# First pair of an attention and gated-MLP kernel rebuilt: keys ahead of values, scores in token halves, q turned by products, x scaled by a diagonal product, one output transfer a tile

## Chip, cores and metric

One core of a Trainium2 chip. The metric is the device time of one execution in microseconds, median of several runs; a run of this kernel can be told from another where they differ by about 0.2%. Engines: PE (TensorE, matrix products; PEld its weight loads), DVE (VectorE), ACT (ScalarE), POOL (GpSimd), SP (SyncE, which issues all DMAs here).

## The reference

```python
def _attn_ref(q, k, v, phi):              # each (8 batches, 8 heads, 576 tokens, 64); phi (.., 32)
    a = np.exp(phi - np.max(phi, axis=2, keepdims=True))
    a = a / (np.sum(a, axis=2, keepdims=True) + 1e-09)
    k_m = np.einsum('bhsm,bhsd->bhmd', a, k)
    v_m = np.einsum('bhsm,bhsd->bhmd', a, v)
    scores = np.matmul(q, k_m.transpose(0, 1, 3, 2)) / np.sqrt(64)
    scores = np.exp(scores - np.max(scores, axis=-1, keepdims=True))
    attn = scores / (np.sum(scores, axis=-1, keepdims=True) + 1e-09)
    return np.matmul(attn, v_m)
...
x = attn_out.transpose(0, 2, 1, 3).reshape(4608, 512)
xn = x / np.sqrt(np.mean(x * x, -1, keepdims=True) + 1e-06) * rms_g
g = xn @ w_gate                            # 512 x 1536, float64 in memory
out = (g / (1 + np.exp(-g)) * (xn @ w_val)) @ w_out
```

Each head has 32 memory slots, so keys and values are first condensed to 32 rows a head; everything after that works on a (tokens x 256 slots of 8 heads).

## The kernel before

**Stages.** Batches go in four pairs. For each batch the kernel makes e = exp(phi - max) (`prep`: maximum mc, two small transposes mt and mr, difference phi, exponential e_bd, partial sums es), then key and value summaries kvp (`kv_steps`: 72 products, the sums, factors si and im, spread tiles kb and vb, turned to kvt and copied as km and vt; vt times rms_g is vm, vt times vt is gram). For each pair it turns q (qtp, copied as qT), makes scores S, subtracts their maximum (mxs, ex), takes exp and divides by the total (sm) to get a. `x_steps` turns a (tp, copied as at), makes sums of squares by way of gram (xp, ssq), inverse norms rinv by Newton steps (`fin`), spreads these over partitions (rp), multiplies at, and splits the product into a high and a low part for exact enough fp32r products (ath, atl).

**Main pass.** 48 columns of 128 hidden units in an order given by ORDER, the first eight for the first pair. A column i has `vw_steps` (vp: weights wc folded with vm, split into xh and xl; the bank of vp is single, so the next vp waits for both xl), `gv_steps` (pg and pv, each three products of high and low parts, for two groups of tokens, 256 and 320 columns; then sg = silu, hf = pv * sg, its high part hh and low part hl), and for each second column `out_steps` (po: six products of 512 columns for each of nine token tiles, added to acc by DVE; when a pair ends, `put` sends acc to memory in two transfers of 64 partitions). "Main pass" below is the time from the first pv or pg on. The weights come as float64 words (raw) and are converted by `convert` on ACT, DVE and POOL (wex, mi, wc, w, oh, ol), then kept in DRAM for later pairs.

**What sets the order.** All steps are small functions in one list, and ISSUE (L31) is a table of their numbers: `perform` calls them in that order, and every engine takes its instructions strictly in that order. Buffers come from pools; a tile whose tag has no free buffer waits for the release of the oldest. Before, L318 loads keys and values of a head pair into one tile (kv, eight buffers), L535 loads all of q of a head pair into the same buffers, and q is copied into another order by ACT (L545) and transposed, nine transposes a head pair. Scores of a head pair take 576 columns in the double bank vw. es is made on POOL (L406), atl too (L778), and hl (L1069).

**Lines used below.** L350 mc, L378 mr, L387 phi, L396 e_bd, L436 kvp products, L448 kvp sums, L472 kb and vb, L487 and L517 kvt, L545 the copy of q, L557 turn of q, L578 S, L591/L595/L606/L612 softmax of the first pair, L665 to L691 that of later pairs, L759 rp, L767 at * rp, L794 xp, L806 squares, L911 to L948 weight conversion, L1002 vp, L1018 xl, L1038 pg and pv, L1054 hf, L1064 hh, L1069 hl, L1095 po, L1104 acc, L1108 output transfers.

## Time and profile before

| | |
|---|---|
| median of 3 runs | 834.62 us (833.40 to 834.71) |
| the profiled execution | 833.51 us, its span 831.7 us, mean granted clock 0.982 |
| busy share | PE 95%, PEld 81%, DVE 55%, ACT 44%, POOL 32% |
| moved by DMA | 120 MB, mean 144 GB/s |
| chain that ended last | PE 84%, DVE 6%, ACT 3%, DMA 3% |

A row of a timeline gives start and duration in us, engine, line, operation, out<-in, shapes, count and in brackets the idle time of the engine before it with what ended it. A row of groups ends with "busy us, mean ns | idle before, and what ended it". PE and PEld overlap, and a row of PE is longer than the spacing of products that follow each other. fp32 products are two records each, transposes and fp32r products one.

### The profile page before, as it was taken

How to read it: one execution, taken by the hardware profiler on the slowest of the kernel's cores; microseconds unless marked ns; L12 is line 12 of the kernel's file. 1: busy time of each engine (PE TensorE's matmuls, PEld its weight loads, DVE VectorE, ACT ScalarE, POOL GpSimd, SP SyncE). 2: the span in 40 equal slices, each digit the busy share in tenths (PEclk: the TensorE clock that was granted, in tenths of full speed). 3: DMA queues.
4: the chain of work that ended last, by engine and by line, in shares of the span. 5: the costliest groups of instructions: out<-in, count | busy, mean ns of one | idle time of the engine just before them, and what ended most of it. 6: DMA issues, size and time to landing. Idle time of an engine off the chain costs nothing.

```text
span 831.7 us, 19077 instructions
## 1 busy us (share of the span) xinstructions
PE 788.9 (95%) x7903; PEld 672.6 (81%) x7903; DVE 459.2 (55%) x1014; ACT 364.0 (44%) x683; POOL 264.7 (32%) x223
## 2 busy tenths in 40 slices
PE   3866999999999999999999999999999999999996
PEld 2654888787988888888888788888888888888884
DVE  4497668899762566555655333556544432444443
ACT  1565688754654646322354247542332244232220
POOL 1255555555542324211153113122241122122220
PEclk9697999999999999999999999999999999999999
DMA  9856677665573450753345454450232433211114
GB/s 322 284 196 223 202 198 220 201 223 197 197 241 102 139 177 21 229 163 110 100 134 171 136 146 109 106 181 32 77 102 73 117 115 127 69 59 52 51 52 114
DMA packets 99327, 120.00 MB, mean 144 GB/s; under 512 B 47908, under 2 KB 64680, under 8 KB 99240
## 3 DMA queue, kind: packets, MB, share of 16 engines
q1 hardware_dynamic: 99240, 118.78, 45.8%
q8 instruction: 62, 1.02, 0.5%
q14 instruction: 25, 0.20, 0.1%
HBM read 93.19 MB, written 25.56 MB: 143 GB/s over the span
## 4 chain that ended last, share of the span: by engine, by line
PE 84%; DVE 6%; ACT 3%; DMA 3%; issue 2%; SPq 1%; POOLq 0%; POOL 0%; DVEq 0%; ACTq 0%
PE po L1095 34%; PE pg L1038 18%; PE pv L1038 17%; PE vp L1002 6%; PE kvp L436 2%; PE xp L794 2%; PE S L665 2%; DMA raw<-in_moe_w_val_dram 1%; PE qtp L647 1%; DMA kv<-in_v_dram 1%; PE tp L739 1%; DVE xl L1018 1%; DVE wex L915 1%; DVE wex L934 1%; DVE mc L350 1%
## 5 line engine op out<-in xcount | busy, mean ns | idle before, releaser
L1069 POOL TENSOR_TENSOR hl<-hf,hh 128x512 fp32r<-128x512 f32 (+1 forms) x96 | 137.9, 1440 | 381.3 <-ACT hh L1064 365.2
L1104 DVE TENSOR_TENSOR acc<-po,acc 128x512 f32<-128x512 f32 x180 | 123.0, 688 | 125.3 <-PE po L1095 124.6
L1095 PE MATMUL po<-oh,hh 128*128 128x512 f32 x432 | 174.9, 405 | 1.8 <-DVE acc L1104 0.9
L1095 PE MATMUL po<-oh,hl 128*128 128x512 f32 x432 | 170.7, 395 | 0.9 <-POOL hl L1069 0.9
L1095 PE MATMUL po<-ol,hh 128*128 128x512 f32 x432 | 170.5, 395 | 0.0
L1049 ACT ACTIVATE sg<-pg 128x256 f32<-128x256 f32 (+1 forms) x192 | 77.3, 412 | 182.4 <-PE pg L1038 148.4
L1054 DVE TENSOR_TENSOR hf<-pv,sg 128x256 f32<-128x256 f32 (+1 forms) x192 | 85.0, 453 | 127.2 <-PE pv L1038 71.7
L1064 ACT CAST hh<-hf 128x512 fp32r<-128x512 f32 (+1 forms) x96 | 64.3, 674 | 80.7 <-DVE hf L1054 79.4
L1095 PEld LDWEIGHTS po<-oh,hh 128*128 128x128 f32 x432 | 81.3, 188 | 22.6 <-issue 3.5
L1095 PEld LDWEIGHTS po<-oh,hl 128*128 128x128 f32 x432 | 81.1, 188 | 21.1 <-POOL hl L1069 1.3
L1095 PEld LDWEIGHTS po<-ol,hh 128*128 128x128 f32 x432 | 81.3, 188 | 14.1
L1038 PE MATMUL pg<-ath,xh 128*128 128x256 f32 (+1 forms) x384 | 87.6, 309 | 0.1
L1038 PE MATMUL pv<-ath,xh 128*128 128x320 f32 (+1 forms) x384 | 86.4, 306 | 0.0
L1038 PE MATMUL pv<-ath,xl 128*128 128x320 f32 (+1 forms) x384 | 82.4, 296 | 0.0
L1038 PE MATMUL pg<-ath,xl 128*128 128x256 f32 (+1 forms) x384 | 82.3, 296 | 0.0
L1038 PE MATMUL pv<-atl,xh 128*128 128x320 f32 (+1 forms) x384 | 82.1, 295 | 0.0
L1020 ACT CAST xh<-vp 128x512 fp32r<-128x512 f32 x96 | 54.5, 587 | 62.5 <-PE vp L1002 30.3
L1038 PE MATMUL pg<-atl,xh 128*128 128x256 f32 (+1 forms) x384 | 81.8, 294 | 0.0
L1018 DVE TENSOR_TENSOR xl<-vp,xh 128x512 fp32r<-128x512 f32 x96 | 64.1, 684 | 30.8 <-ACT xh L1020 30.8
L1038 PEld LDWEIGHTS pg<-ath,xh 128*128 128x128 f32 x384 | 63.1, 189 | 11.7 <-issue 4.2
L1038 PEld LDWEIGHTS pv<-ath,xh 128*128 128x128 f32 x384 | 64.1, 190 | 9.4 <-issue 2.3
L1038 PEld LDWEIGHTS pv<-atl,xh 128*128 128x128 f32 x384 | 61.8, 189 | 0.0
(114 smaller groups left out, 1079.7 us busy)
## 6 DMA issues: line engine op xcount, KB each, us to landing
wc<-wd SPq DMA_DIRECT2D x36, 512.0 KB, 4.4
oh<-od SPq DMA_DIRECT2D x36, 256.0 KB, 3.6
ol<-od SPq DMA_DIRECT2D x36, 256.0 KB, 4.0
out_dram<-acc SPq DMA_DIRECT2D x72, 128.0 KB, 3.0
kv<-in_k_dram SPq DMA_DIRECT2D x26, 288.0 KB, 6.1
kv<-in_v_dram SPq DMA_DIRECT2D x26, 288.0 KB, 6.0
qr<-in_q_dram SPq DMA_DIRECT2D x48, 144.0 KB, 3.4
raw<-in_moe_w_val_dram SPq DMA_DIRECT2D x12, 512.0 KB, 3.9
```

What stands on the lines that cost most here:

```text
L436: nc.tensor.matmul(st["kvp", b][cc][to, 0:128], e_of(b)[rows, hp, c, :], st["kv", b, hp][rows, :, 64 * c:64 * c + 64], start=(c == 0), sto ...
L665: nc.tensor.matmul(sp[64 * j:64 * j + 64, 64 * t:64 * t + 64], d["qT"][:, t0 + t, 64 * j:64 * j + 64], st["km", 2 * pr + j][:, s, :], star ...
L1002: nc.tensor.matmul(vp[32 * g:32 * g + 32, flip(b, cc), cc, :], vm[pr][rows, b, hp, 32 * (g % 2):32 * (g % 2) + 32], w[rows, hp, :], start= ...
L1018: V.tensor_tensor(out=xl[:, k], in0=src, in1=xh[:, k].bitcast(F32), op=ALU.subtract)
L1020: nc.scalar.copy(xs[i][0][:, k], src)
L1038: nc.tensor.matmul(pt[:, :N], l[:, flip(b, cc), cc, half * P:half * P + P], r[:, b, cc, t0:t0 + n, :].rearrange("p t x -> p (t x)"), start ...
L1049: nc.scalar.activation(sg[:, :N], acts[gi, b, 0][:, :N], AF.Silu)
L1054: V.tensor_tensor(out=acts[gi][:, :, b, :], in0=acts[gi, b, 1][:, :N].rearrange("p (t x) -> p t x", x=64), in1=acts[gi, b, 2][:, :N].rearr ...
L1064: nc.scalar.copy(hh, acts[gi].rearrange("p t b x -> p t (b x)"))
L1069: nc.gpsimd.tensor_tensor(out=hl, in0=acts[gi].rearrange("p t b x -> p t (b x)"), in1=hsplit[i, gi][0].bitcast(F32), op=ALU.subtract,)
L1095: nc.tensor.matmul(po, l[:, tt, :], r, start=(m == 0), stop=(m == 5))
L1104: V.tensor_tensor(out=accs[key], in0=pt[0], in1=accs[key], op=ALU.add)
```

## The change

Seven edits and a new table:

1. Keys and values of the first pair are loaded and multiplied apart (`load_one`, `kv_steps(b, i)`): keys of both batches first, values later. Factors si and im are made once with the keys (`scale_all`); hmask is laid out for that.
2. q of the first pair is loaded, turned and scored in two parts of the tokens, tiles 0 to 3 and 4 to 8. A turn is no transpose of a reordered copy any more, but two plain products with the identity for each token tile, one for each head, into halves of the partitions. Scores take one bank of tag g for each part.
3. x of the first pair isn't multiplied by spread norms: `scaled` makes diagonal tiles dg of the norms on ACT, multiplies a by them on PE (ts), and splits the bank directly (ath on ACT, atl on DVE). The other pairs keep the old way.
4. es of the first two batches on DVE instead of POOL.
5. hl of the second token group of the first twelve columns on DVE instead of POOL.
6. The first two raw weight blocks have buffers of their own.
7. One output transfer of 128 partitions a tile instead of two of 64.

The ISSUE table is new throughout.

```diff
-    10, 11, 0, 12, 1, 13, 2, 14, 15, 16, 3, 4, 5, 6, 900, 7, 27, 8, 17, 9, 29, 30, 31, 32, 33, 34, 38, 18, 19,
...
+    def load_one(i, b, hp):
+        t = sa.tile([P, S], F32, tag="kv", name=f"{'kv'[i]}{b}_{hp}", bufs=9)
+        load(t, (k, v)[i][b, 2 * hp:2 * hp + 2].rearrange("h (p c) d -> (h p) (c d)", c=NT))
+        st["kv"[i], b, hp] = t
...
-                nc.gpsimd.tensor_tensor(
+                (V if b < 2 else nc.gpsimd).tensor_tensor(
                     out=t, in0=e[:, :, 0:2, :] if c == 2 else t, in1=e[:, :, c:c + 2, :], op=ALU.add
...
+        products = [chunk(c, c + 3) for c in range(0, NT, 3)]
+        if i == 0:
+            return products + [sums, scale_all(), spread(0), spread(1)], [turn(0), put_k]
+        if i == 1:
+            return products + [spread(0), spread(1)], [turn(1), [put_v, gain], self_products, keep]
...
-                    nc.tensor.transpose(
-                        out=tp[:, (t - t0) * P:(t - t0 + 1) * P],
-                        in_=qr[:, t].rearrange("p h d -> p (h d)"), identity=ident,
-                    )
+                    for h in range(2):
+                        nc.tensor.matmul(
+                            tp[64 * h:64 * h + 64, (t - t0) * P:(t - t0 + 1) * P],
+                            qr[:, h, 64 * t:64 * t + 64], ident, start=True, stop=True,
+                        )
...
-            sp = ps.tile([P, 1024], F32, tag="vw", name=f"S0_{s}", bufs=1)
-            for t in range(NT):
+            sp = bank("g", f"S0_{s}_{t0}")
+            for t in range(n):
...
+        def scaled(t0):
+            n = min(2, NT - t0)
+            def diag(t):
+                def f():
+                    d["dg", t] = dg = sa.tile([P, P], F32, tag="dg", name=f"dg{t}", bufs=4)
+                    nc.scalar.activation(dg, ident, AF.Copy, scale=rinv[pr][:, t:t + 1])
+                return f
+            def mm():
+                tps["s", t0] = tp = bank("v", f"ts{pr}_{t0}")
+                for t in range(t0, t0 + n):
+                    for cc in range(2):
+                        o = 2 * (t - t0) + cc
+                        nc.tensor.matmul(
+                            tp[:, o * P:(o + 1) * P], srcs[t][:, cc * P:(cc + 1) * P], d["dg", t],
+                            start=True, stop=True,
+                        )
...
-                nc.gpsimd.tensor_tensor(
+                (V if gi and i < 12 else nc.gpsimd).tensor_tensor(
                     out=hl, in0=acts[gi].rearrange("p t b x -> p t (b x)"),
...
-                for b in range(2):
-                    load(
-                        out[(2 * pr + b) * S:(2 * pr + b + 1) * S].rearrange("(p c) d -> p c d", c=NT)[:, t, :],
-                        accs[key0, t][64 * b:64 * b + 64, :],
-                    )
+                load(
+                    out[2 * pr * S:(2 * pr + 2) * S].rearrange("(q c) d -> q c d", c=NT)[:, t, :],
+                    accs[key0, t],
+                )
...
+    for t0, n in GROUPS:
+        for s in range(HP):
+            add(lambda s=s, t0=t0, n=n: load_q(s, t0, n), q_steps(s, t0 == 0), score_steps(s, t0, n))
+    for b in range(2):
+        add([lambda b=b, hp=hp: load_one(1, b, hp) for hp in range(HP)], *kv_steps(b, 1))
```

The order at three places. First DVE where the scores of the first pair begin, before; the number after a name's first digits tells the head pair, and the last number is the buffer's.

```order
L934 SCALAR_TENSOR_TENSOR wex0_0_459<-raw_00_314,wex0_0_459 128x512
L350 TENSOR_REDUCE mc2_0_546<-phi2_456 128x128
L591 TENSOR_REDUCE mxs0_0_559<-S0_0_523 128x18
L595 TENSOR_TENSOR ex0_0_561<-S0_0_523,mxs0_0_559 128x576
L365 TENSOR_REDUCE mx2_0_564<-mt2_0_548 128x2
L373 COPY mb2_0_568<-mx2_0_564 128x128
L606 TENSOR_REDUCE sm0_0_574<-ex0_0_561 128x18
L591 TENSOR_REDUCE mxs0_1_610<-S0_1_578 128x18
```

DVE at the same place after; the third number of mxs, S and ex is the first token tile of the part.

```order
L491 TENSOR_TENSOR kb1_473<-kvp1_0_319,im1_444 128x128 x2
L491 TENSOR_TENSOR vb0_601<-kvp0_1_476,im0_402 128x128
L640 TENSOR_REDUCE mxs0_0_0_603<-S0_0_0_569 128x8
L644 TENSOR_TENSOR ex0_0_0_605<-S0_0_0_569,mxs0_0_0_603 128x256
L491 TENSOR_TENSOR vb0_601<-kvp0_1_476,im0_402 128x128
L640 TENSOR_REDUCE mxs0_1_0_633<-S0_1_0_589 128x8
L644 TENSOR_TENSOR ex0_1_0_635<-S0_1_0_589,mxs0_1_0_633 128x256
L653 TENSOR_REDUCE sm0_0_0_661<-ex0_0_0_605 128x8
```

The scores follow the summaries of the keys at once; weight conversions and the maximum of batch 2 (mc2) have moved behind them.

Second PE where the main pass begins, before; kvp3 is the summary of batch 3, mr3 a transpose of its prep.

```order
L517 MATMUL kvt2_1091<-vt2_1113 64x64 x4
L1002 MATMUL vp2_1141<-wc2_1002,vm0_469 32x256 x16
L378 MATMUL mr3_0_1165<-ident_72,mb3_0_1058 128x128
L1038 MATMUL pv0_10_1170<-ath0_1103,xh0_847 128x320 x2
L1038 MATMUL pv0_10_1170<-atl0_1108,xh0_847 128x320 x2
L1038 MATMUL pv0_10_1170<-ath0_1103,xl0_882 128x320 x2
```

PE there after.

```order
L462 MATMUL kvp3_0_1346<-ones_109,e_bd1_131 32x1 x4
L462 MATMUL kvp3_1_1347<-ones_109,e_bd1_131 32x1 x4
L1090 MATMUL vp1_1480<-wc1_1208,vm0_639 32x256 x16
L1126 MATMUL pg0_00_1510<-ath0_1152,xh0_1387 128x256 x2
L1126 MATMUL pg0_00_1510<-atl0_1163,xh0_1387 128x256 x2
L1126 MATMUL pg0_00_1510<-ath0_1152,xl0_1393 128x256 x2
```

All of kvp3 now stands ahead of the main pass, vp2 behind its first products. On DVE the last operations that these wait for are now the following, with mc4, the maximum of batch 4, among them.

```order
L864 TENSOR_TENSOR atl0_1163<-ts0_4_1328,ath0_1152 128x2x128 x2
L359 TENSOR_REDUCE mc4_0_1372<-phi4_1308 128x128
L1106 TENSOR_TENSOR xl0_1393<-vp0_1189,xh0_1387 128x512
L864 TENSOR_TENSOR atl0_1163<-ts0_6_1378,ath0_1152 128x2x128
L1106 TENSOR_TENSOR xl0_1393<-vp0_1189,xh0_1387 128x512
```

Before, neither atl nor mc4 was on this list of DVE at this place.

Third PE near the end, before: the last pv of column 47 stands between two output tiles.

```order
L1095 MATMUL po47_3_10188<-oh47_10143,hl47_0_10154 128x512
L1038 MATMUL pv47_11_10200<-ath3_7814,xh47_9931 128x320 x2
L1038 MATMUL pv47_11_10200<-atl3_7963,xh47_9931 128x320 x2
L1038 MATMUL pv47_11_10200<-ath3_7814,xl47_9933 128x320 x2
L1095 MATMUL po47_5_10214<-oh46_10158,hh46_1_10094 128x512
```

PE near the end after.

```order
L1126 MATMUL pv47_11_10397<-ath3_8037,xl47_10210 128x320 x2
L1126 MATMUL pv47_10_10404<-ath3_8037,xh47_10208 128x320 x2
L1126 MATMUL pv47_10_10404<-atl3_8055,xh47_10208 128x320 x2
L1126 MATMUL pv47_10_10404<-ath3_8037,xl47_10210 128x320 x2
L1183 MATMUL po47_0_10413<-oh46_10357,hh46_0_10273 128x512
```

All pg and pv of the last column now stand ahead of its nine output tiles.

More of the change, by code (lines that the diff above doesn't have):

```diff
@@ L864, in x_steps @@
         steps.append(fin(4, NT))
+        if pr == 0:
+            return steps + [scaled(t0) for t0 in range(0, NT, 2)]
         for t0, n in ((0, 4), (4, 4), (8, 1)):
@@ L891, in load_w @@
         j = column(n)
-        t = wp.tile([P, 512, 2], I32, tag="raw", name=f"raw_{kind}{n}", bufs=2)
+        if n < 1 and kind < 2:
+            t = sa.tile([P, 512, 2], I32, tag="raw0", name=f"raw_{kind}{n}", bufs=2)
+        else:
+            t = wp.tile([P, 512, 2], I32, tag="raw", name=f"raw_{kind}{n}", bufs=2)
         if kind == 2:
@@ L1125 @@
     load(st["rg_rows"], rms_g.rearrange("(hp r) -> hp r", r=P))
-    for hp in range(HP):
-        load_kv(0, hp)
     load_phi(1)
-    for hp in range(HP):
-        load_kv(1, hp)
+    for b in range(2):
+        for hp in range(HP):
+            load_one(0, b, hp)
     add(prep(0, 0, 2), prep(0, 2, 4)[:-1], prep(1))
```

168 lines of the change are left out of this document (105 added, 63 removed), and 320 rows, old and new, of the table ISSUE.

## The prediction

> **What bounds the kernel now.** I read the windows first, then the order of time in the two places where TensorE is not full: the head and the last 20 us. The columns are the stretch, its length, busy time of PE, PEld, DVE, ACT and POOL, the granted clock, the DMA share and GB/s.
>
> ```profile
> 0.00:37.15 37.15, 20.25 (x455) 15.78 (x456) 16.58 (x53) 12.31 (x19) 8.64 (x16) 0.81 0.86 296
> 37.15:79.20 42.05, 28.38 (x544) 20.57 (x545) 38.50 (x112) 24.93 (x49) 20.46 (x19) 0.87 0.68 229
> 79.20:208.00 128.80, 125.78 (x1272) 106.88 (x1273) 102.50 (x220) 87.54 (x162) 72.29 (x60) 0.99 0.67 206
> 208.00:811.00 603.00, 601.31 (x5581) 519.45 (x5580) 294.91 (x620) 238.50 (x455) 161.73 (x128) 1.00 0.38 117
> 811.00:831.70 20.70, 13.22 (x57) 9.91 (x55) 6.72 (x10) 0.72 (x1) 1.55 (x1) 0.92 0.50 114
> ```
>
> Between 79.2 and 811 us PE idles 3.0 + 1.7 us: the main pass is bound by TensorE, and nothing in this change takes products out of it. The head (0 to 79.2) holds 30.6 us of idle PE and the tail 7.5. So the span is the start of the main pass, plus the products left then, plus the tail.
>
> The head has two stretches. Up to 37.15 DMAs bring phi, keys, values and q (296 GB/s), and the first maximum of scores waits for them. From there VectorE is busy 38.5 of 42.05 us. These rows of the timeline are the two borders:
>
> ```profile
> 37.15 0.76 DVE L591 TENSOR_REDUCE mxs<-S 128x18 f32<-128x576 f32 x1 [1.90 <-PE S L578]
> ```
>
> ```profile
> 79.20 0.88 PE L1038 MATMUL pv<-ath,xh 128*128 128x320 f32 x2
> ```
>
> **The change part by part.** *The scores start earlier.* Before, the first scores stand behind sixteen key and value transfers, two weight blocks and all of q 0. The weight block of 512 KB issued behind phi (2 x 576 KB) and the sixteen (288 KB each) ends ScalarE's wait here:
>
> ```profile
> 23.56 0.67 ACT L911 ACTIVATE wex<-raw 128x512 f32<-128x512 f32 x1 [2.46 <-DMA raw<-in_moe_w_val_dram]
> ```
>
> That is 6272 KB by 23.5 us, 267 KB/us from zero. After, the first scores need both batches' keys, the first half of q 0 and, since PE takes them in order, the values of batch 0. Up to the last of these SP issues 1152 of phi, 8 x 288 of keys, 4 x 256 + 320 of q and 4 x 288 of values: 5952 KB, at 22.3 us. Then PE runs the 72 value products of batch 0, one turn of q and the turn of the keys of batch 1:
>
> ```profile
> 20.55 1.12 PE kvt L487 x4
> 21.67 4.29 PE kvp L436 x141
> ```
>
> The 141 records of 128 columns took 4.29 us; 144 of 64 columns cost between half of that and all of it. I take 2.2 (the columns halve), plus 0.6 for two of four kvt, plus 1.2 for eight products of the turn (below), plus 0.3 for scores: 22.3 + 4.3 = 26.6 us, so 26.5, between 25 and 28.5. Before it was 37.15.
>
> *The turn of q.* The copy L545 goes; it runs on ScalarE, busy 24.9 of 42 us, and costs nothing once the scores have begun. A turn is now two plain products into 64-partition halves instead of one transpose. The nearest row is xp, with the same shape (72 records are 36 products):
>
> ```profile
> L557 PE MATMUL qtp<-ident,qr 128*128 128x128 f32 x36 | 8.1, 359 | 1.8 <-ACT qT L563 1.8
> ```
>
> ```profile
> L794 PE MATMUL xp<-gb,at 128*64 128x128 f32 x72 | 5.3, 282 | 3.1 <-DVE ssq L806 1.7 <-ACT at L749 1.4
> ```
>
> A product is 5.3 / 36 = 0.147 us, 72 of them 10.6 against 8.1: 2.5 us more, in PE time that idles; if the idle were gone, 2.5 us later. Eight of them are 1.2 us on the path, counted above.
> The Trainium skill speaks against this edit: TensorE: Matmul & The Clock Gate, section Terms, calls the transpose mode 4 times faster for FP32, and TensorEngine Tiling (Array Packing), section Restrictions, says that column tiling turns it off. By that an eighth of the turns, 0.9 us as transposes, would cost 3.6 instead of 1.2, the scores would start 2.4 us later, and the sum below would be 8.3 instead of 10.7; the xp row puts the ratio for this shape at 10.6 / 8.1, and I use the row.
>
> *VectorE's list from the first maximum to the start of the main pass.* Before, it ends with the product of x and the spread norms (L767), at 76.1. After, PE's last product ahead of the main pass, vp1, needs the bank of vp0, so it waits for the second xl0. Between these borders the two lists differ, at these means of 37.15 to 76.1:
>
> ```profile
> L934 DVE SCALAR_TENSOR_TENSOR wex<-raw,wex 128x512 int32<-128x512 int32 x6 | 4.6, 761 | 0.0
> L806 DVE CUSTOM_DVE_ANT_0 xp<-xp,a 128x256 f32<-128x256 f32 x9 | 3.7, 433 | 0.0
> L915 DVE TENSOR_SCALAR wex<-wex 128x512 f32<-128x512 f32 x7 | 3.5, 513 | 1.0 <-ACT wex L911 0.9
> L591 DVE TENSOR_REDUCE mxs<-S 128x18 f32<-128x576 f32 x4 | 3.0, 756 | 1.9 <-PE S L578 1.9
> L595 DVE TENSOR_TENSOR ex<-S,mxs 128x576 f32<-128x576 f32 x4 | 3.0, 752 | 0.1
> L606 DVE TENSOR_REDUCE sm<-ex 128x18 f32<-128x576 f32 x4 | 3.0, 748 | 0.9 <-ACT ex L602 0.8
> L927 DVE TENSOR_SCALAR wex<-wex 128x512 int32<-128x512 int32 x7 | 2.9, 414 | 0.0
> L1018 DVE TENSOR_TENSOR xl<-vp,xh 128x512 fp32r<-128x512 f32 x4 | 2.7, 685 | 0.0
> L767 DVE TENSOR_TENSOR at<-at,rp 128x1024 f32<-128x1024 f32 x2 | 2.4, 1214 | 0.7 <-PE rp L759 0.7
> L350 DVE TENSOR_REDUCE mc<-phi 128x128 f32<-128x1152 f32 x1 | 2.1, 2130 | 0.0
> ...
> L387 DVE TENSOR_TENSOR phi<-phi,mr 128x1152 f32<-128x1152 f32 x1 | 1.3, 1294 | 0.0
> ...
> L612 DVE RECIPROCAL sm<-sm 128x18 f32<-128x18 f32 x4 | 1.1, 263 | 0.1
> ```
>
> Halves of scores, and a difference that VectorE now takes from a bank, cost as in the later pairs:
>
> ```profile
> L677 DVE TENSOR_REDUCE mx<-S 128x10 f32<-128x320 f32 x12 | 5.9, 492 | 10.7 <-PE S L665 10.5
> ```
>
> ```profile
> L677 DVE TENSOR_REDUCE mx<-S 128x8 f32<-128x256 f32 x12 | 5.1, 424 | 2.8 <-PE S L665 1.9
> L472 DVE TENSOR_TENSOR vb<-kvp,im 128x128 f32<-128x128 f32 x16 | 4.5, 283 | 0.1
> ```
>
> Added: the maxima mc2 and mc4 (2 x 2.13 = 4.3), the difference phi3 (1.3), seven atl differences of 256 columns (3.0 at 0.424; on GpSimd before), the splitting of four score groups into eight (maxima and differences 8 x 0.16 = 1.3, small operations 8 x 0.2 = 1.6), three more vb (0.85): 12.3. Gone: two products with the norms (2.4), four of the 20 wex operations (2.2), one xl (0.7): 5.3. Net 7.0 us more. VectorE took 38.95 us from 37.15 to 76.1; after it takes 38.95 + 7.0, and vp1 1.0. The main pass starts at 26.5 + 45.95 + 1.0 = 73.5 instead of 79.2: **5.7 us**. Ends: VectorE's 3.5 us of idle squeezed out and scores at 25 give 68.5; scores at 28.5 and 4 us of waits for late transfers (phi4 and the last of the keys and values of batch 3 are issued behind weight conversions) give 79.5. The sums es move from GpSimd to VectorE ahead of the scores, where it is busy 16.6 of 37 us: nothing, or 1 us inside those ends.
>
> *Products done before the main pass.* Before, the 144 records of kvp3 lie in it, after they lie ahead of it; vp2 goes the other way. From the chain:
>
> ```profile
> 82.47 0.87 PE kvp L436 x48
> ```
>
> ```profile
> 93.78 0.47 PE kvp L448 x38
> 94.25 0.99 PE vp L1002 x32
> ```
>
> 3 x 0.87 plus 0.47 for the sums, less 0.99: **2.1 us** less is left.
>
> *Inside the main pass.* The twelve hl of 640 columns of the first twelve columns go from GpSimd to VectorE, at
>
> ```profile
> L1069 POOL TENSOR_TENSOR hl<-hf,hh 128x640 fp32r<-128x640 f32 x48 | 75.8, 1580 | 177.7 <-ACT hh L1064 168.9 <-DVE hf L1054 8.8
> ```
>
> 1.58 us on GpSimd, and by xl's 0.685 for 512 about 0.86 on VectorE: 10.3 us, beside 26.3 idle us of VectorE in 79.2 to 208 and more later. I take 0; from 3 us gained (PE's whole idle there) to 4 lost.
>
> *The tail.* Before, one pv of the last column stands between two output tiles, and the next tile waits twice:
>
> ```profile
> 818.15 0.50 PE L1095 MATMUL po<-oh,hh 128*128 128x512 f32 x1 [0.76 <-ACT hh L1064]
> 818.49 0.39 PE L1095 MATMUL po<-ol,hh 128*128 128x512 f32 x1
> 819.78 0.50 PE L1095 MATMUL po<-oh,hl 128*128 128x512 f32 x1 [0.90 <-POOL hl L1069]
> ```
>
> After, all pv precede the tiles, and four tiles cover hf, hh and hl: **1.7 us** gone. Then SP issues two transfers a tile:
>
> ```profile
> 825.92 0.69 DVE L1104 TENSOR_TENSOR acc<-po,acc 128x512 f32<-128x512 f32 x1 [0.70 <-PE po L1095]
> ```
>
> ```profile
> 825.25 3.68 SPq L1108 DMA_DIRECT2D out_dram<-acc  x6
> ```
>
> Six issues take 3.68, 0.61 each; the last begins at 828.3, 1.7 after the last sum ends at 826.6. With one issue a tile it begins at once. A transfer of twice the size lands later, by at most the difference of
>
> ```profile
> out_dram<-acc SPq DMA_DIRECT2D x18, 128.0 KB, 2.4
> oh<-od SPq DMA_DIRECT2D x2, 256.0 KB, 3.3
> ```
>
> So 0.8 to 1.7 us; I take **1.2**.
>
> The sum: 5.7 + 2.1 + 0 + 1.7 + 1.2 = 10.7 us. The profiled execution took 833.5 us (span 831.7 and 1.8 around it), the median of the three runs is 834.6; 834.6 - 10.7 = 823.9.
>
> **The rivals.** *The head does not shorten*: the scores are early, but phi4, mc4 and the transfers of batch 3 stand between, and the main pass starts at 79.2 again. For it speaks that DMA share is 0.68 there with SP waiting for buffers; against it that VectorE's own list already reaches 73. Then 2.1 + 1.7 + 1.2 = 5.0 remain: 829.6.
> *The head shortens more*: VectorE's idle and the waits between halves vanish, and the main pass starts at 67: 12.2 + 5.0 = 17.2, 817.4. For it: all engines but VectorE idle a third of the time or more. Against: 3.5 us are all that VectorE has to give, the rest must come from earlier scores.
> *Slower: VectorE becomes the bound of the main pass's first columns.* The twelve hl land where VectorE is busy 102.5 of 128.8 us, and tiles (acc), hf and xl queue behind each of them in order. If one hl costs on VectorE what it costs on GpSimd, twelve are 19 us, and with the 2.2 of conversions left over, in the six or so columns where it is already nearly full, PE waits for most of it. It decides from 10.7 us of waits on, that is 0.9 us for each hl; with 13 us the time is 837. Against it: 26.3 idle us, and xl's row.
>
> **How the numbers follow.** Chances: forecast 0.56, head unchanged 0.17, head shorter still 0.16, VectorE bound 0.11. The range reaches from 812 (the second rival, 3 us gained in the main pass, the tail's best 0.5 and scores at 25 instead of 26.5) to 832 (the forecast with the head at 79.5 and 2 us of waits on hl); the third rival lies outside it. No change within 0.2% (1.7 us) is 0.05, the edge between the first and the third rival; slower 0.10, faster 0.85.
>
> **What would show it.** Right: the first maximum at about 26.5, the main pass at about 73.5, no wait of po for hh or hl in the last 15 us, SP's last issue at once behind the last sum. Wrong: first scores later than 29, a main pass that starts behind a DMA (mc4 or kvp3), or PE waiting over 4 us in all for acc, xl or hf between the start of the main pass and 250 us.

## The result, and the profile after

The change made the kernel slower: 838.66 us (836.29 to 841.23, nine runs) beside 833.40 us (831.02 to 834.71, nine runs), a ratio of 1.0066 [1.0049, 1.0084]. The prediction was 823.9. The profiled execution took 841.23 us (span 839.5), 2.6 above its median; that of before took 833.51 (span 831.7).

The windows of after, cut at the start of its main pass (85.55), and, as the middle row, from the first maximum of scores to the end of the second xl. Columns: stretch, length, busy time of PE, PEld, DVE, ACT and POOL, granted clock, DMA share, GB/s.

```profile
0.00:85.55 85.55, 59.10 (x1581) 47.83 (x1581) 57.08 (x187) 34.15 (x75) 20.65 (x30) 0.90 0.71 230
29.65:83.75 54.10, 40.77 (x901) 33.59 (x897) 43.06 (x136) 27.71 (x65) 19.48 (x23) 0.84 0.64 206
85.55:836.00 750.45, 743.32 (x6750) 634.00 (x6745) 412.69 (x873) 329.96 (x622) 220.42 (x173) 1.00 0.43 133
```

The main pass of before, in the same view:

```profile
79.20:826.00 746.80, 740.31 (x6906) 636.24 (x6906) 403.51 (x849) 326.76 (x616) 235.57 (x189) 1.00 0.43 132
```

So the head grew by 6.35 us, the main pass by about 3.5, and the end behind the last product fell from 5.8 to 3.7: 6.35 + 3.5 - 2.1 = 7.8, the difference of the spans (the medians differ by 5.3). In the head PE is busy for 10.4 us more (48.6 to 59.1) and idle for only 4.1 less.

The two borders of the prediction, in the timeline of after: the first maximum came at 29.65 instead of 37.15 and the main pass at 85.55 instead of 79.20.

```profile
29.65 0.42 DVE L640 TENSOR_REDUCE mxs<-S 128x8 f32<-128x256 f32 x1 [0.32 <-PE S L630]
```

```profile
85.55 0.50 PE L1126 MATMUL pg<-ath,xh 128*128 128x256 f32 x2
```

So the scores are 7.5 us earlier, and the 55.9 us from there to the main pass take 13.9 more than the 42.05 of before. VectorE is busy for 43.06 of the 54.10 us and idle for 11.04. Its waits in that stretch (total, times, longest):

```profile
DVE mxs L640 <- PE S L630: 3.4, 5, 1.1
DVE vb L491 <- PE kvp L450: 3.3, 1, 3.3
DVE atl L864 <- ACT ath L868: 2.1, 2, 1.2
```

With two smaller waits, 7.9 of these 11.0 us are waiting for PE. And PE itself stands at places where it waits for nothing that the profile shows ("issue"). In the timeline of after, these four rows:

```profile
16.95 2.01 PE L450 MATMUL kvp<-k,e_bd 64*32 64x64 f32 x123 [1.87 <-issue]
...
21.23 0.36 PE L462 MATMUL kvp<-ones,es 64*32 64x1 f32 x23 [1.88 <-issue]
...
41.35 0.86 PE L450 MATMUL kvp<-v,e_bd 64*32 64x64 f32 x42 [2.65 <-issue]
...
83.78 0.32 PE L450 MATMUL kvp<-kv,e_bd 64*32 64x128 f32 x5 [1.43 <-issue]
```

They come to 7.8 us, all amid the smallest products of the kernel. Two lie ahead of the first scores. The third holds up VectorE directly, in the timeline of DVE:

```profile
42.27 0.29 DVE L491 TENSOR_TENSOR vb<-kvp,im 128x128 f32<-128x128 f32 x1 [3.34 <-PE kvp L450]
```

The fourth ends at 83.78, just as the last xl0 ends on VectorE (83.75). vp1 had to wait for that xl0 in any case, so the stop put off only the rest of kvp3, by these rows some 0.7 us (83.78 to 84.47, where vp1 begins): not all of the 7.8 us lies on the path. Before has one such stop of note, and a small one (0.54):

```profile
28.57 0.30 PE L436 MATMUL kvp<-kv,e_bd 64*32 64x128 f32 x2 [2.61 <-issue]
```

At the end of the span the change did what it said: no po waits for hh or hl any more, and SP's nine issues, one a tile, are through at 836.87, 0.4 us behind the end of the last sum (836.51).

```profile
825.34 11.53 SPq L1195 DMA_DIRECT2D out_dram<-acc  x9
```

```profile
835.82 0.69 DVE L1192 TENSOR_TENSOR acc<-po,acc 128x512 f32<-128x512 f32 x1 [0.71 <-PE po L1183]
```

### The profile page after: what moved, and what is told of

It reads as the page before. It is cut to its first block, busy times and chain, and to the rows that moved or that the text cites. A ratio compares the mean times of both kernels' runs of the same rounds, so it can differ in the third digit from the quotient of the medians.

```text
span 839.5 us, 19946 instructions
## 1 busy us (share of the span) xinstructions
PE 802.4 (96%) x8326; PEld 681.8 (81%) x8326; DVE 470.3 (56%) x1060; ACT 364.1 (43%) x696; POOL 241.1 (29%) x203
## 3 DMA queue, kind: packets, MB, share of 16 engines
q8 instruction: 65, 1.06, 0.5%
## 4 chain that ended last, share of the span: by engine, by line
PE 87%; DVE 5%; DMA 3%; ACT 2%; issue 2%; SPq 0%; ACTq 0%; DVEq 0%
PE po L1183 34%; PE pg L1126 18%; PE pv L1126 18%; PE vp L1090 5%; PE kvp L450 2%; PE xp L877 2%; PE S L711 2%; DMA raw<-in_moe_w_val_dram 1%; PE qtp L693 1%; PE qtp L608 1%; DVE mc L359 1%; PE tp L785 1%; DMA qr<-in_q_dram 1%; DMA raw<-in_moe_w_gate_dram 1%; PE kvt L533 1%
## 5 line engine op out<-in xcount | busy, mean ns | idle before, releaser
L1157 POOL TENSOR_TENSOR hl<-hf,hh 128x512 fp32r<-128x512 f32 (+1 forms) x84 | 120.2, 1431 | 373.5 <-ACT hh L1152 342.0
L1183 PEld LDWEIGHTS po<-ol,hh 128*128 128x128 f32 x432 | 81.3, 188 | 13.2
L1126 PE MATMUL pv<-ath,xh 128*128 128x256 f32 (+1 forms) x384 | 87.8, 310 | 0.0
L1126 PE MATMUL pv<-ath,xl 128*128 128x256 f32 (+1 forms) x384 | 82.2, 295 | 0.0
L1126 PE MATMUL pv<-atl,xh 128*128 128x256 f32 (+1 forms) x384 | 82.2, 295 | 0.0
L1126 PEld LDWEIGHTS pg<-ath,xh 128*128 128x128 f32 x384 | 63.6, 189 | 12.2 <-issue 3.9
L1126 PEld LDWEIGHTS pg<-ath,xl 128*128 128x128 f32 x384 | 62.0, 189 | 1.3 <-issue 1.3
```

The costliest lines, as they stand in the source:

```text
L1126: nc.tensor.matmul(pt[:, :N], l[:, flip(b, cc), cc, half * P:half * P + P], r[:, b, cc, t0:t0 + n, :].rearrange("p t x -> p (t x)"), start ...
L1157: (V if gi and i < 12 else nc.gpsimd).tensor_tensor(out=hl, in0=acts[gi].rearrange("p t b x -> p t (b x)"), in1=hsplit[i, gi][0].bitcast(F ...
L1183: nc.tensor.matmul(po, l[:, tt, :], r, start=(m == 0), stop=(m == 5))
```

## Experiments

Several explanations were tried. **A, transfers**: the reordered preparation of batch 2 releases its phi buffer late, so that SP, which waits for it, issues nothing meanwhile, and late data lengthen the head. **B, ScalarE**: weight conversions stand ahead of the first sg and hh, and ScalarE waits for raw blocks. **C, hl on VectorE**, the rival on record. **D, the diagonal product**: it lengthens the chain from the last norm to the main pass; **E** is its rival, the late place of xh and xl of column 0. **F, TensorE's own list** bounds the head; with it goes the question whether the many tiny products of the new head cost their work alone, or more than their busy time because their instructions cannot be supplied that fast. **G, VectorE's list** bounds the head, as the prediction had it. Differences to after are differences between ratios to before, times 833 us. A fence that begins with "ISSUE" shows moves in the order table.

### Transfers, the tail, hl and conversions

A rests on this row of SP's waits in after (total, times, longest):

```profile
SPq L318 <- ACT e_bd L405: 16.1, 2, 13.6
```

`e1_prep2` puts the preparation of batch 2, its sums and its key and value products behind the first halves of the scores, so that SP has a phi buffer in time.

```diff
 ISSUE
-134, 121, 271, 122, 135 ... 190, 272, 273, 191 ... 148, 205, 276, 211 ... 277, 207, 278, 285, 199
+127, 104, 271, 272, 105 ... 106, 117, 273, 274, 275 ... 142, 276, 277, 118 ... 148, 278, 279, 280 ... 189, 285, 286, 287
```

> The changed kernel with one thing moved: the preparation of batch 2 (its maximum, its two turns, the difference, the exponential, its sums and its products with keys and values) stands behind the first halves of the scores instead of behind the last ones. Theory A (the place of that preparation): in the changed kernel the maximum of batch 2 runs at 51.4 us instead of 33.1, VectorE idles before it, and SyncE, which holds the load of phi 3 ahead of all other loads, issues nothing from 45.4 to 59.0. Then here SyncE's pause falls from 13.7 us to under 7, the main pass starts 3 to 6 us earlier than 85.6, and the time falls by 3 to 6 us below the changed kernel's 838.7. Theory B (ScalarE's list: weight conversions that wait for their transfers stand ahead of the hi halves, the sigmoids and hh): the order of ScalarE stays, the time moves by less than 1.5 us. Theory C (the twelve hl on VectorE): no change over 1 us.

Measured: 840.72 us, 1.0102 [1.0079, 1.0126]: 3.0 ± 2.4 us above after. SP's pause only moved, to the weight blocks; this is SP's longest wait there:

```profile
SPq L992 <- DVE wex L1032: 17.2, 2, 14.3
```

The main pass began at 89.46. A falls in this form: freeing the phi buffer did not shorten the head.

`e2_before_tail` is before, with the last pv ahead of the output tiles and one transfer a tile: the tail of the change alone.

```diff
 ISSUE
-2915, 2916, 2902, 2911, 2901, 2903, 2914, 2904, 2905, 2921
+1264, 2900, 2901, 2895, 2899, 2902, 2903, 2904, 2905, 1262
...
-                for b in range(2):
-                    load(
-                        out[(2 * pr + b) * S:(2 * pr + b + 1) * S].rearrange("(p c) d -> p c d", c=NT)[:, t, :],
-                        accs[key0, t][64 * b:64 * b + 64, :],
-                    )
+                load(
+                    out[2 * pr * S:(2 * pr + 2) * S].rearrange("(q c) d -> q c d", c=NT)[:, t, :],
+                    accs[key0, t],
+                )
```

> The kernel before with the two edits of the tail alone: the last pv products stand ahead of the last column's output tiles, and each output tile leaves in one transfer. By the prediction's steps 1.7 + 1.2 = 2.9 us less than before (2.5 to 3.4); if the waits of po were hidden anyway or the larger transfer lands later by as much as it saves, 0 to 1.2.

Measured: 828.07 us, 0.9942 [0.9924, 0.9961], 4.8 us (3.2 to 6.3) below before: this version beats both kernels. Its last rows are those of after:

```profile
811.72 11.53 SPq L1116 DMA_DIRECT2D out_dram<-acc  x9
```

```profile
822.20 0.69 DVE L1113 TENSOR_TENSOR acc<-po,acc 128x512 f32<-128x512 f32 x1 [0.71 <-PE po L1104]
```

`e3_hl_pool` gives hl of the first twelve columns back to GpSimd.

```diff
-                (V if gi and i < 12 else nc.gpsimd).tensor_tensor(
+                nc.gpsimd.tensor_tensor(
```

> The changed kernel with the twelve hl of 640 columns back on GpSimd. Theory C (the rival of the prediction that ended slower): 3 us or more less than the changed kernel, and TensorE's waits from 85 to 250 us fall. Theories A and B: within 1.7 us of it, because one hl costs 0.81 us on VectorE (first one in the trace) and VectorE idles a fifth of that stretch.

Measured: 838.10 us, 1.0059 [1.0043, 1.0076], no difference to after (-0.6 ± 2.0). C falls. The group of the twelve hl in after shows that they cost little and waited for 0.5 us in all:

```profile
L1157 DVE TENSOR_TENSOR hl<-hf,hh 128x640 fp32r<-128x640 f32 x12 | 12.1, 1005 | 0.5 <-ACT hh L1152 0.5
```

`e4_act` moves three groups of weight conversions behind the first sg and hh.

```diff
 ISSUE
-262, 267, 1011, 1327 ... 1351, 1333, 1033, 1338 ... 1340, 1341, 1027, 1029 ... 1354, 1015, 1034, 487, 1028
+1340, 1341, 1011, 1009, 1010, 1012, 1013, 1033 ... 1345, 1346, 1027, 1029, 1034, 1028, 1030 ... 488, 336, 1031, 1032
```

> The changed kernel with the conversions of the weights of columns 2 (value part) and 3 moved behind the first sigmoids and hh in every engine's list, and the load that reuses their buffer behind them. Theory B: ScalarE's two waits for weight transfers ahead of the last hi half and of the first hh (2.57 and 2.72 us) go, TensorE loses less from 85 to 112 us, 3 to 5 us less than the changed kernel. Theory A: the main pass still starts at about 85 us, and the weights of column 2 are only late in another place: between 1.5 us less and 3 us more.

Measured: 842.92 us, 1.0114 [1.0095, 1.0133]: 4.0 ± 2.2 us above after. The main pass began at 83.94, but the windows show PE busy for only 21.55 of the 26.06 us behind that:

```profile
83.94:110.00 26.06, 21.55 (x221) 18.00 (x217) 17.29 (x39) 17.12 (x33) 9.06 (x8) 0.87 0.61 170
```

B falls in this form: an earlier start was given back at once.

### Where the stops of TensorE sit

The stops have a pattern. The instruction queue of the page (packets, MB, share) has 65 packets in after, of 1.06 / 65 = 16 KB each; TensorE has 8326 products and as many weight loads:

```profile
PE 802.4 (96%) x8326; PEld 681.8 (81%) x8326; DVE 470.3 (56%) x1060; ACT 364.1 (43%) x696; POOL 241.1 (29%) x203
...
q8 instruction: 65, 1.06, 0.5%
```

16652 / 65 = 256 instructions a packet. In before it is 15806 / 62 = 255. Counting all instructions of TensorE's stream in the trace, the four stops of after lie behind 449, 705, 1729 and 3009 instructions. Each is 193 beyond a multiple of 256. That suggests blocks of 256 instructions, and a stop wherever TensorE has run through a block before the next is there.

`e5_pad` puts 64 one-column products ahead of the first product, to shift the program against this grid.

```diff
             st["mt", key] = tp = bank("o", f"mt{b}_{hp0}")
+            if key == (0, 0):
+                for _ in range(64):
+                    nc.tensor.matmul(tp[:1, 256:257], ones, ones, start=True, stop=True)
```

> The changed kernel with 64 products of one column (128 instructions) ahead of TensorE's first product, in time that idles. If TensorE's stops that wait for nothing the profile shows are ends of blocks of 256 instructions that have to be fetched (in the changed kernel they stand at instructions 449, 705, 1729 and 3009 of its stream, 256 or a multiple apart), each moves by 128 instructions of the program, to another place. If they belong to the place (DMA queues full of keys and values), they stay at the same products.

Measured, in one run: 842.58 us. The page counts 8454 products, 128 more, with as many loads: 256 instructions, a whole block, so the program did not shift within the grid, and what followed is no test of it. Stops stayed in the key products and the sums; the one in the value products shrank to 0.22 us, and another came two blocks earlier, in the turn of q, where e3 has one too without any padding:

```profile
17.80 2.01 PE L463 MATMUL kvp<-k,e_bd 64*32 64x64 f32 x123 [1.79 <-issue]
...
33.71 0.27 PE L621 MATMUL qtp<-ident,q 128*64 128x128 f32 x1 [2.62 <-issue]
```

The test came with the next run, which takes out 216 instructions.

`e6_copy` turns q as before: a copy on ScalarE and one transpose a tile, 36 records instead of 144.

```diff
+            nc.scalar.copy(qr, src)
...
-                    for h in range(2):
-                        nc.tensor.matmul(
-                            tp[64 * h:64 * h + 64, (t - t0) * P:(t - t0 + 1) * P],
-                            qr[:, h, 64 * t:64 * t + 64], ident, start=True, stop=True,
-                        )
+                    nc.tensor.transpose(
+                        out=tp[:, (t - t0) * P:(t - t0 + 1) * P],
+                        in_=st["qr", s, g0][:, t - g0].rearrange("p h d -> p (h d)"), identity=ident,
+                    )
```

> The changed kernel with q put in order by a copy on ScalarE again and turned by one transpose a tile (36 records) instead of two plain products (144 records). Theory F: 216 instructions and some 3 to 4 us of work leave TensorE between 22 and 46 us, where it is busy without a pause but for instruction waits; the last scores end 2 to 4 us earlier, and the time falls by 1.5 to 4 us. Theories D and E: what VectorE does behind the scores decides, and the time stays within 1.5 us of the changed kernel. By the rule that a transpose is four times faster, the turns would fall from 10.8 us to under 3.

Measured: 834.99 us, 1.0031 [1.0007, 1.0054]: 2.9 ± 2.5 us below after. Its third stop lies again behind 1729 instructions, though that is now another line of the program:

```profile
44.52 0.39 PE L573 MATMUL kvt<-vt 128*64 128x64 f32 x5 [2.07 <-issue]
```

The stops are tied to the count of instructions, not to an operation. In the first 80 us of all nineteen kernels traced, 63 stops of half a microsecond or more end in "issue", and each lies 193 beyond a multiple of 256. Their sizes vary: where TensorE's stream is the same up to there, the stop behind 1729 instructions took 1.1 us in one profile (e4) and 3.5 in another (e13), and one behind 1217 came in some and not in others. So a single stop is weak evidence; their place, and sums over a head, are better.

The traces also hold the time of every packet of the instruction queue, and these settle what the stops wait for. Count the boundary behind 449 instructions as the first; then 705 is the second, 1729 the sixth and 3009 the eleventh. In after the first, second, sixth and eleventh packet landed at 15.49, 19.96, 39.95 and 82.41 us, and the four stops ended at 16.95, 21.23, 41.35 and 83.78, 1.3 to 1.5 us behind them. All 63 stops end 1.2 to 1.6 us behind the landing of the packet with their boundary's number, and none of the other 114 boundaries in these 80 us was passed sooner than 1.2 us behind its packet. So TensorE stands there for its next 256 instructions. When a packet sets out varies, up to 4.7 us after TensorE passed the boundary before; what decides that is open.

### The diagonal product

`e8_spread_late` and `e9_spread_early` take the scaling of x by spread norms from before; the second moves parts of the main pass's start forward as well. In both, the tile a and the bank of rp of the first pair change their buffers too.

```diff
-        if pr == 0:
-            return steps + [scaled(t0) for t0 in range(0, NT, 2)]
```

> The changed kernel with x of the first pair scaled as before (the norms are spread by transposes into a bank, VectorE multiplies the turned x, GpSimd makes the lo half), but xh and xl of column 0 still behind the last scaling. Theory D (the diagonal product lengthens the chain from the last norm to the main pass: 75.2 to 85.6 us in the changed kernel, 73.4 to 79.2 before): 3 to 5 us less than the changed kernel. Theory E (not the product but the place of xh and xl of column 0 behind it, whose space is that of the first pair's tiles, 80 to 84 us instead of 55 to 58): within 1.5 us of it.

> As the run with the scaling of before, and the first pair's tiles are given up right after the conversion of column 0, so that xh and xl of columns 0 and 1 stand ahead of the last scaling, as before. Theory D: as that run, within 1.5 us. Theory E: a further 3 to 6 us less, main pass starting before 80 us. Theory F (TensorE and its supply of instructions bound the stage of the scores): the main pass starts at most 3 us earlier and the time stays within 3 us of the changed kernel's 838.7.

Measured: 846.02 us, 1.0162 [1.0134, 1.0189], and 846.31 us, 1.0160 [1.0135, 1.0185]. Both say nothing on the product: the new order put sums on GpSimd ahead of PE, which waited for them, in the first of the two for 7.92 us:

```profile
88.78 0.42 PE L471 MATMUL kvp<-ones,es 64*32 64x1 f32 x32 [7.92 <-POOL es L424]
```

`e18_spread_early2` is the second with these sums issued earlier.

```diff
 ISSUE
-1336, 956, 298, 243, 245 ... 957, 958, 299, 995, 306 ... 307, 949, 300, 308, 989
+973, 297, 298, 299, 300, 974, 227
```

> As the run with the scaling of before and the early xh and xl, with the sums of batch 3 ahead of the lo halves in GpSimd's list, so that its new wait (5.9 us of TensorE) is gone. If the diagonal product is worth nothing, the time is the changed kernel's 838.7 within 1.5 us; if it gains by itself, 840 or more; if it costs (theories D and E), 836 or less.

Measured: 840.96 us, 1.0088 [1.0067, 1.0108], 1.8 ± 2.3 us above after. By its median that falls into the branch where the diagonal product gains by itself (840 or more), but the interval holds "worth nothing" as well: the 2.7 us that D and E wanted at the least are not there, and a gain is not shown.

### One engine's work at a time

Four runs add work to after's head, to see whose time counts.

`e10_pe_work` puts five whole products ahead of each later turn of q (40 records):

```diff
+                if t0 == 4:
+                    for _ in range(5):
+                        nc.tensor.matmul(tp[:, :P], ident, ident, start=True, stop=True)
```

> The changed kernel with 20 more products of 128x128 on TensorE (40 instructions), five ahead of each turn of the second halves of q, between 31 and 42 us; by the product of ts in the trace (0.17 us) some 3.4 us more. Theory F (TensorE's list bounds the head): 2 to 4 us slower than the changed kernel. Theory G (VectorE's list bounds it, the prediction's own assumption): within 1 us, because the products lie in TensorE's idle time.

`e11_pe_instr` puts 32 small ones there (256 records):

```diff
+                if t0 == 4:
+                    for _ in range(32):
+                        nc.tensor.matmul(tp[:32, :64], ident[:64, :32], ident[:64, :64], start=True, stop=True)
```

> The changed kernel with 128 tiny products of 32x64 on TensorE (256 instructions, one more block), 32 ahead of each turn of the second halves of q; at 7 to 16 ns each 1 to 2 us of work. If the supply of instructions counts by itself, the cost is that of a block, 3 to 4 us, and one more stop appears between 30 and 45 us; if only work counts, 1 to 2 us by theory F and nothing by theory G.

`e12_dve_work` sums the exponentials of the scores twice:

```diff
             V.tensor_reduce(out=d["sm"], in_=d["ex"], axis=AX.X, op=ALU.add)
+            V.tensor_reduce(out=d["sm"], in_=d["ex"], axis=AX.X, op=ALU.add)
```

> The changed kernel with every sum of exponentials of the first pair taken twice on VectorE: 4 x 0.40 + 4 x 0.48 = 3.5 us more in its list between 31 and 54 us. Theory G: 3 to 4 us slower than the changed kernel. Theory F: at most 1.5 us slower, because VectorE idles 11 us from the first maximum to the main pass.

`e13_act_work` makes the copies qT of the later halves twice:

```diff
+                for _ in range(1 + (t0 > 0)):
```

> The changed kernel with the copies of the turned second halves of q made twice on ScalarE: 4 x 0.58 + 4 x 0.25 = 3.3 us more in its list between 34 and 47 us. Theories F and G: within 1 us of the changed kernel. If ScalarE's list is what holds the scores, 2 to 3 us slower.

Measured: e10 (PE) 841.39 us, 1.0093 [1.0069, 1.0116], +2.3 ± 2.4 on after; e12 (3.5 us on DVE) 839.59, 1.0082 [1.0057, 1.0107], +1.3 ± 2.5; e13 (3.3 us on ACT) 839.87, 1.0073 [1.0056, 1.0090], +0.6 ± 2.0. None can be told from nothing, and the forecasts of F and of G both lie within these intervals, so these three decide nothing between the engines. e11 was to add instructions without work and failed at that: 849.33, 1.0189 [1.0170, 1.0209], +10.3 ± 2.2, but the products, all on one tile of the array, took 15.0 us instead of the 1 to 2 expected:

```profile
L618 PE MATMUL qtp<-ident 64*32 64x64 f32 x256 | 15.0, 216 | 0.0
```

### Instructions without work

`e14_tiny` adds 128 one-column products to after, spread over four tiles of the array: 512 instructions.

```diff
+                if t0 == 8:
+                    for x in range(32):
+                        h, g = x % 2, x % 4
+                        nc.tensor.matmul(
+                            tp[32 * g:32 * g + 32, 256 + x:257 + x], ident[64 * h:64 * h + 64, :32],
+                            ident[64 * h:64 * h + 64, :1], start=True, stop=True,
+                        )
```

> The changed kernel with 128 products of one column on 64x32 tiles more (256 records, 512 instructions, two more blocks of 256), 32 ahead of each turn of the last token tile of q, where TensorE is busy; by the sums of the kv products (10 ns a record) 2 to 3 us of work. If only work counts (theory F): 1 to 2.5 us slower than the changed kernel. If the supply of instructions counts by itself: the stops that wait for nothing grow by 3 to 6 us between 30 and 50 us and the time by 3 to 7 us. Theory G (VectorE's list bounds the head): within 1 us.

Measured: 847.40 us, 1.0162 [1.0133, 1.0192], 8.0 ± 2.9 us above after. Their group is busy for 3.4 us:

```profile
L619 PE MATMUL qtp<-ident 64*32 64x1 f32 x256 | 3.4, 174 | 0.6 <-issue 0.6
```

The main pass began at 93.42, 7.9 us later than in after, and the windows of the head read

```profile
0.00:93.42 93.42, 65.08 (x1837) 52.12 (x1837) 57.47 (x188) 34.53 (x76) 20.64 (x30) 0.87 0.66 213
```

PE is idle for 28.3 us instead of 26.5 and busy for 6.0 more: 3.4 are the new products, and most of the rest is the turn of q (14.7 us instead of 12.2), at a granted clock of 0.87 instead of 0.90 in the head. So the price is more than twice the work added, though only 1.9 us of it are idle time, and the claim that the supply costs stops alone is not borne out here.

`e15_before_plain` makes q's turn in before by two plain products a tile: 216 instructions more.

```diff
-                    nc.tensor.transpose(
-                        out=tp[:, (t - t0) * P:(t - t0 + 1) * P],
-                        in_=qr[:, t].rearrange("p h d -> p (h d)"), identity=ident,
-                    )
+                    for h in range(2):
+                        nc.tensor.matmul(
+                            tp[64 * h:64 * h + 64, (t - t0) * P:(t - t0 + 1) * P],
+                            qr[:, t, h], ident, start=True, stop=True,
+                        )
```

> The kernel before with one part of the change: q of the first pair is turned by two plain products a tile instead of one transpose (the copy stays, nothing else moves): 144 records instead of 36, 216 instructions and 3 to 4 us more for TensorE ahead of the main pass. Theory F: 2 to 4 us slower than before. Theory G, the prediction's: it lies in TensorE's idle time, within 1 us.

Measured: 833.80 us, 1.0001 [0.9984, 1.0018]. In before's order this is free, as the idle time of PE there covers it.

`e16_before_split` does to before what the change does to the products of the first two batches: keys and values in 64 columns each, all of a batch's keys first. Nothing else changes, and no transfer moves.

```diff
+                        if b < 2:
+                            continue
...
+                for i, c in [(i, c) for i in range(2) for c in range(NT)][6 * (c0 // 3):6 * (c0 // 3) + 6] if b < 2 else ():
+                    for cc, hp, rows, to in tiles():
+                        nc.tensor.matmul(
+                            st["kvp", b][cc][to, 64 * i:64 * i + 64],
+                            e_of(b)[rows, hp, c, :],
+                            st["kv", b, hp][rows, i, 64 * c:64 * c + 64],
+                            start=(c == 0), stop=(c == NT - 1),
+                        )
```

> The kernel before with one part of the change: keys and values of batches 0 and 1 are multiplied in separate products of 64 columns (all key products of a batch ahead of its value products), nothing else moves: 288 records and 576 instructions more for TensorE ahead of the first scores, by the changed kernel's trace some 3 us of work. Theory F: 2 to 4 us slower than before; theory G: within 1 us, since TensorE idles two thirds of that stretch.

Measured: 843.64 us, 1.0127 [1.0097, 1.0158]: 10.6 us (8.1 to 13.2) slower than before, for 2.2 us more of busy PE in the span (791.1 beside 788.9). That is far above the expectations of F and of G. The work of the products is not it: those of keys and values in the head, these 576 records and 108 of batch 2 (2.8 us), are busy for 12.6 us, beside 12.4 in before:

```profile
L436 PE MATMUL kvp<-kv,e_bd 64*32 64x128 f32 x396 | 12.4, 366 | 4.9 <-issue 2.6 <-ACT e_bd L396 1.4 <-DMA kv<-in_v_dram 0.9
```

```profile
L455 PE MATMUL kvp<-kv,e_bd 64*32 64x64 f32 x576 | 9.8, 310 | 11.9 <-issue 9.5 <-ACT e_bd L405 1.4 <-DMA kv<-in_k_dram 1.1
```

The timeline shows the stops:

```profile
19.25 1.23 PE L455 MATMUL kvp<-kv,e_bd 64*32 64x64 f32 x68 [3.97 <-issue]
31.73 2.04 PE L455 MATMUL kvp<-kv,e_bd 64*32 64x64 f32 x128 [3.82 <-issue]
35.46 0.68 PE L455 MATMUL kvp<-kv,e_bd 64*32 64x64 f32 x32 [1.69 <-issue]
...
65.02 0.81 PE L758 MATMUL tp<-ident,a 128*128 128x128 f32 x6 [2.25 <-issue]
```

These four come to 11.7 us, beside 3.2 in before; the head's busy PE grew by 2.2 (50.8 beside 48.6). And this is what became of the two borders, which were 37.15 and 79.20:

```profile
44.58 0.76 DVE L610 TENSOR_REDUCE mxs<-S 128x18 f32<-128x576 f32 x1 [2.11 <-PE S L597]
```

```profile
88.95 0.88 PE L1057 MATMUL pv<-ath,xh 128*128 128x320 f32 x2
```

So the main pass starts 9.75 us later, and the additional stops add up to 8.6 of it. This edit alone costs more than the whole change lost. Its stops lie behind 449, 961, 1217 and 2241 instructions: the last of them, behind all 576 additional instructions (two and a quarter blocks), still sits on the grid.

`e17_few_values` is after with the value products of the first pair for the first of nine token chunks only: it leaves out eight ninths of the values of that pair, 256 records and 512 instructions.

```diff
-                for c in range(c0, c1):
+                for c in range(c0, c1) if i != 1 else range(c0, 1):
...
-                            start=(c == 0), stop=(c == NT - 1),
+                            start=(c == 0), stop=(c == (0 if i == 1 else NT - 1)),
```

> The changed kernel with the value products of batches 0 and 1 left out for all token chunks but the first (256 records, 512 instructions, some 3 us of work less; the values of the first pair are then sums over a ninth of the tokens). If the supply of instructions bounds TensorE ahead of the main pass: its stops that wait for nothing fall from 7.9 us to under 5 and the time by 5 to 9 us, to 830 to 834. If only their work counts (theory F): 1 to 3 us less. Theory G: within 1 us of the changed kernel.

Measured: 830.80 us, 0.9977 [0.9961, 0.9993]: 7.4 ± 2.0 us below after, and now below before. Two stops are left:

```profile
16.53 2.01 PE L460 MATMUL kvp<-k,e_bd 64*32 64x64 f32 x123 [0.77 <-issue]
...
21.08 0.35 PE L472 MATMUL kvp<-ones,es 64*32 64x1 f32 x23 [2.15 <-issue]
```

Their sum fell by 4.9 us. The first maximum came at 28.02 and the main pass at 78.22, 7.3 earlier than in after. The windows from the first maximum to the end of the second xl, and of the head:

```profile
28.02:77.14 49.12, 38.64 (x834) 31.60 (x830) 42.91 (x136) 27.58 (x65) 19.46 (x23) 0.86 0.71 235
0.00:78.22 78.22, 54.80 (x1325) 43.96 (x1325) 56.99 (x187) 34.20 (x76) 20.63 (x30) 0.91 0.77 253
```

VectorE does the same work as in after (42.9 us) and is idle for 6.2 instead of 11.0. This run takes out work as well as instructions (PE's head is busy for 4.3 us less), so it does not part the two by itself; e16 does, in before's order.

## Why the prediction was wrong, step by step

*First scores at 26.5 (25 to 28.5): wrong, 29.65.* The transfers were foretold well: the last values of batch 0 landed at 22.42 (22.3 in the sum). What was too small is the 4.3 us of TensorE's work behind them. TensorE is busy from 22.40 on without a pause, and the scores begin 6.5 us later; these rows stand in that list, with the value products (2.45 us, priced at 2.2) and the turn of the keys of batch 1 (0.6, as priced) between:

```profile
22.40 1.98 PE L608 MATMUL qtp<-ident,q 128*64 128x128 f32 x16
...
26.72 1.60 PE L608 MATMUL qtp<-ident,q 128*64 128x128 f32 x16
...
28.90 0.70 PE L630 MATMUL S<-km,qT 128*64 128x64 f32 x16
```

Two turns of q, 1.9 and 1.5 us to the next product, stand where the sum has one of 1.2: 2.2 of the 3.15 us. The list also began late, behind two stops of 1.87 and 1.88 us that no step had; how much earlier the scores would have come without them was not tried.

*The turn of q, 2.5 us more "in PE time that idles": the size was near, the cover was not.* In before's order (e15) the turn costs nothing; its group reads

```profile
L567 PE MATMUL qtp<-ident,qr 128*64 128x128 f32 x144 | 10.8, 298 | 1.4 <-ACT qT L573 1.4
```

beside the 8.1 us of before, 2.7 more. In after itself the turn is busy for 12.2 us, 4.1 more, and taking it back gained 2.9 ± 2.5. "If the idle were gone, 2.5 us later" was the branch that held. The Trainium skill, TensorE: Matmul & The Clock Gate, section Terms, gives transposes four times the speed for FP32. These rows give 10.8 / 8.1 = 1.33, so the measurement decides against the factor of 4 for this shape; that the edit is against the kernel is true, by a smaller sum. (The 0.9 us that the prediction set beside it are a ninth of the turns, 8 of 72 products, not an eighth.)

*VectorE's list, main pass at 73.5: the step that failed.* The count of VectorE's work was right: 35.96 busy before plus 7.0 is 42.96, and 43.06 was measured. That it fits to 0.1 is in part luck: there were eight atl where seven were counted and two xl fewer where one was, and before's list really ended at 77.09, with a third product with the norms (0.42 us), not at 76.1. What failed was to carry the idle time of before (3.0 us) over to a list with eight groups of scores from PE instead of four, while PE got 10.4 us more to do in the head. VectorE idled for 11.04 us, mostly waiting for S (3.4) and for the value products (3.3, behind the third stop). From 29.65, 43.06 + 11.04 gives 83.75, and the rest of kvp3 and vp1 lead to 85.55. The premise behind it, that PE has 30.6 idle us in the head and takes any addition there, was wrong: many of those microseconds were waits for others on a chain, and additions to PE in the new order lay on that chain.

The loss comes with one edit above all, the splitting of the first pair's keys and values into separate products: it doubles the number of instructions for the same columns. Put into before alone it costs 10.6 us, most of it in stops in which TensorE waits for its next packet of instructions (e16); with most of the value products left out, after is faster than before (e17). What is not settled is how much of after's own 6.35 us are stops (7.8 us in its head beside 3.2) and how much is work on the chain (PE is busy for 10.4 us more: the turn of q takes 12.2 instead of 8.1, the diagonal product 6.4 where spreading the norms took 2.2, and kvp3 has moved ahead): the two overlap, and e10, e12 and e13 were too close to after to part them. Even then the earlier scores brought little. In e17 the first maximum is 9.1 us earlier than in before, and the main pass 1.0: of those 9.1 us, 7.0 go to what VectorE has more to do, 3.2 to what it idles more, and 2.0 came back behind the list.

*Products of kvp3 done before the main pass, 2.1 us: they were, but the main pass did not get shorter.* With the po waits it should have fallen by 3.8 and it rose by 3.5. In its first 24.45 us PE idles for 2.85, where before has 0.15, and the granted clock is 0.93 instead of 0.97:

```profile
85.55:110.00 24.45, 21.60 (x228) 18.11 (x224) 16.54 (x40) 17.27 (x35) 11.06 (x9) 0.93 0.71 202
```

Over the whole main pass PE idles for only 0.6 more (7.1 beside 6.5), since the po waits are gone; the rest is 3.0 us more of busy PE with fewer records, which no single line holds. The profiled execution of after is itself 2.6 us above its median, so part of this can be that execution's own. e4 aimed at this stretch and made it worse. This part stays open.

*hl on VectorE, taken as 0: right.* It took 1.0 us each instead of 0.86, and the time does not change without it (e3: -0.6 ± 2.0).

*The tail, 1.7 + 1.2: right in kind, and the second term too small.* The po waits are gone, and the span now ends 3.7 us behind the last product instead of 5.8: 2.1 less, where 1.2 was taken and 1.7 was the most. e2 gives 4.8 us (3.2 to 6.3) for both together, beside 2.9 forecast; its profiled head was 1.6 us shorter than that of before, with no edit there, so the surplus need not be the tail's.

*The rivals.* Unchanged head and shorter head were both out: the head became longer. The slower rival's 837 was near, its mechanism (hl) was not at work. A rival in which PE's additions lay on the path was missing.

## What to carry to other kernels

Idle time of an engine in a stretch where engines take turns is no cover: ask of each microsecond whom that engine was waiting for, and whether the added work stands ahead of the next hand-over. Price TensorE's small products by their number as well as by their columns: splitting one product into two of half the width doubles the instructions. And take an edit apart before adding it up: here the tail alone was worth 4.8 us (3.2 to 6.3), and the rebuilt head lost more than that. Where an engine stands and nothing is seen to release it, count its instructions up to there and look at the packets of the instruction queue.

## What the runs showed of the hardware

TensorE's instructions came in packets of 16 KB, 256 instructions each, and TensorE stood for 0.5 to 4.0 us at positions 193 beyond a multiple of 256, mostly amid tiny products, until 1.2 to 1.6 us after the next packet had landed. By differences, 512 additional instructions of 3.4 us of work cost 8.0 ± 2.9 us (e14), 576 that made PE's head 2.2 us busier cost 10.6 (e16), and 216 cost nothing where TensorE waited for others anyway (e15). What decides when the next packet sets out was not tried.

Tiny products of one shape differ in price: 256 records of 64 columns on a single 64 x 32 tile took 15.0 us (e11), 59 ns each, and 288 of the same shape that go round the tiles (the value products of after) 5.0 us, 17 ns each. Those of e11 also write the same 32 x 64 words of a bank each time, so the tile need not be the cause.
